# The causal mask of the row maxima moves from VectorE's reduction into a second bf16 product on TensorE

## The chip, the core and the metric

The program runs on one core of a Trainium2 chip. A core has a matrix engine (TensorE, PE in the profile, whose weight loads are the row PEld), VectorE (DVE), ScalarE (ACT), GpSimd (POOL) and a DMA-issuing engine (SP). Matrix products are written to PSUM, of which this kernel uses eight banks of 128 partitions by 512 fp32 numbers. The metric is the device time of one execution in microseconds (us). The kernel before takes 1426.77 us, the median of three runs that lie between 1425.55 and 1429.22 us.

## The reference

Two stages follow each other. The first is causal attention over 8 batches of 8 heads, with 576 positions and 64 numbers a head, and a decay that is summed along the sequence:

```python
scores = scale * np.matmul(q, k.transpose(0, 1, 3, 2))
bias = -(cum[:, :, :, None] - cum[:, :, None, :])
scores = np.where(causal, -1000000000.0, scores + np.minimum(bias, 0.0))
scores = scores - np.max(scores, axis=-1, keepdims=True)
attn = np.exp(scores)
attn = attn / (np.sum(attn, axis=-1, keepdims=True) + 1e-09)
return np.matmul(attn, v).astype(np.float32)
```

The second mixes the attention's output x with the real part of a two-dimensional Fourier transform, normalises each row, and applies a two-layer network with a hidden width of 2048:

```python
u = x + mixed
un = (u - mu) / np.sqrt(var + 1e-06)
ch = np.maximum(un @ w_ch1, 0.0) @ w_ch2
return (u + ch).astype(np.float32)
```

The change concerns one line of the first stage: the maximum of each row over the positions that the causal mask leaves.

## The kernel before

**Attention.** The 64 heads are worked in 32 steps of two heads (`i` in the loop at L585). Each step has several streams. `load` and `high` (L418, L420) and `low` (L435 on VectorE, L438 on GpSimd) split q and k into a rounded part and a remainder. `maxes` (L446 to L475) computes the rows' maxima, `scores` (L479 to L502) the exponentials with the maximum already subtracted, and `av` (L506 to L533) the product with v. `recip` and `finish` divide by the sums. For every fourth step a batch is complete, and `folds` (L244 to L268, mainly VectorE and GpSimd) and `fourier` (L274 to L342, mainly TensorE) mix it. A share of the weight conversion (`rounded`, L74 to L91) runs beside all this.

**The maxima.** For each head, the 576 query rows are cut into five blocks c of 128 rows (the last has 64). Block c needs the keys up to its own last row, so its product (L459) has 256, 256, 384 and 512 columns for c = 0 to 3; the last block has two products, of 256 and 320 columns. Each product goes into one of five PSUM buffers of the pool `psm`, which the products of `av` and the transposition of the maxima (L471) share. VectorE then reduces each buffer to one column. Where the product holds the diagonal block, a fused operation (L466) adds a mask from `amask`, writes the masked row to `trash`, and keeps the maximum in an accumulator, which a second instruction reads out into a column of `M` (`Mx` in the profile). The mask tile `amask` has 512 columns of zeros and then a 128 x 128 triangle with -1e30 above the diagonal; its window is placed so that the triangle meets the diagonal. Of the last block's two products, the first has no diagonal: a plain maximum (L462) puts it into `M1`, and that number is the starting value of the second one's accumulator. The ten columns of `M` are transposed on TensorE (L471), copied by ScalarE (L473), and sent by a DMA (L474) into row 2 of the query tile `qy`, where the products of `scores` (L491) read them.

**What sets the order.** `weave` and `mixed` (L702 to L717) take the next piece from the stream that is furthest behind its share, so the order in which the program issues is fixed when it is built. From L584 to L639 TensorE's order is exactly that order. On the other engines the framework's planner places the instructions. Each engine then runs its own queue in order and stops at an instruction whose semaphore has not come. Where `low` overwrites `k1`, VectorE waits at L435 until the last product of `scores` that reads it (L492) is done.

**Network.** After attention come the last folds, the rest of the weight conversion and the first normalisation; then nine token tiles (`mlp_tile`, L164) run products of 512 columns (L183, L196 to L198).

Of the kernel before, what the change touches and what calls it, by code (L numbers as in the profile page):

```python
# [8 lines left out]
F32 = mybir.dt.float32  # L9
F32R = mybir.dt.float32r  # L10
AF = mybir.ActivationFunctionType
ALU = mybir.AluOpType
BF16 = mybir.dt.bfloat16
I32 = mybir.dt.int32
U16 = mybir.dt.uint16
AX = mybir.AxisListType
# [9 lines left out]
NEG = -1.0e30  # L26
# [15 lines left out]
def fused_kernel(ctx, tc, qkT, vA, sP, wP, tabD, tabS, corr, out):  # L42
    nc = tc.nc
# [14 lines left out]
    ident = const.tile([128, 128], F32, name="ident")  # L58
# [289 lines left out]
    att = att_ctx.enter_context(tc.tile_pool(name="att", bufs=1, side="right"))  # L348
# [39 lines left out]
    Ms = [att.tile([128, 10], F32, name=f"Mx{i}") for i in range(2)]  # L388
    for M in Ms:
        nc.vector.memset(M, 0.0)  # L390
    amask = att.tile([128, 640], BF16, name="amask")
    nc.gpsimd.memset(amask, 0.0)
    nc.gpsimd.affine_select(out=amask[:, 512:640], in_=amask[:, 512:640], pattern=[[-1, 128]], compare_op=ALU.is_ge, fill=NEG, base=0, channel_multiplier=1)
    trash = att.tile([128, 512], BF16, name="trash")
    for i in range(1, NR):
        fixed_rows(i, nc.gpsimd, nc.gpsimd)

# [48 lines left out]
    def maxes(i):  # L446
        st = sts[i]
        qy, ky = st["qy"], st["ky"]
        M = Ms[i % 2]
        M1 = att.tile([128, 4], F32, tag="M1", name="M1", bufs=2)  # L450
        for h in range(2):
            for c in range(5):
                nq = 128 if c < 4 else 64
                nk = 128 * c + nq
                parts = [(0, max(nk, 256))] if c < 4 else [(0, 256), (256, 320)]
                col = M[:nq, 5 * h + c:5 * h + c + 1]
                for x, (k0, n) in enumerate(parts):
                    p = psm.tile([128, 512], F32, tag="m", name="pm", bufs=5)
                    nc.tensor.matmul(p[:, :n], qy[:, h, 128 * c:128 * c + 128], ky[:, h, k0:k0 + n], start=True, stop=True)  # L459
                    if len(parts) > 1 and not x:  # L460
                        first = M1[:nq, h:h + 1]
                        nc.vector.tensor_reduce(out=first, in_=p[:nq, :n], axis=AX.X, op=ALU.max)  # L462
                    else:
                        n = nk - k0
                        m0 = 512 - 128 * c + k0
                        nc.vector.tensor_tensor_reduce(out=trash[:nq, :n], in0=p[:nq, :n], in1=amask[:nq, m0:m0 + n], scale=1.0,  # L466
                                                       scalar=first if x else NEG, op0=ALU.add, op1=ALU.max, accum_out=col)
                    yield 1.0
        yield 3
        p = psm.tile([128, 512], F32, tag="m", name="pmt", bufs=5)  # L470
        nc.tensor.transpose(out=p[0:10, 0:128], in_=M, identity=ident)  # L471
        mt = att.tile([10, 128], F32R, tag="mt", name="mt", bufs=2)
        nc.scalar.copy(mt, p[0:10, 0:128])  # L473
        nc.sync.dma_start(out=qy[2:3].bitcast(F32).rearrange("o h (c t) -> o (h c) t", t=128), in_=mt.bitcast(F32))  # L474
        yield 1.0  # L475
# [95 lines left out]
    weave([high(0), 1])  # L571
    cum_rows()
    weave([low(0), 1], [high(1), 1], [maxes(0), 1.0])
    weave([low(1), 1], [high(2), 1], [maxes(1), 1.0])
    mixing = None
    weights = convert_w(attb, 0, NC, 1)
# [8 lines left out]
    for i in range(NP):  # L585
# [5 lines left out]
        if 2 <= i + 1 < NP:  # L591
            streams.append([maxes(i + 1), MAXES / 0.7])
            streams.append([later(low(i + 1), i % 4 == 0), (6, 7, 4, 3)[i % 4]])
# [69 lines left out]
    op = None  # L663
# [149 lines left out]
```

## Time and profile before

| what | value |
|---|---|
| median of three runs | 1426.77 us (1425.55 to 1429.22) |
| profiled execution | 1426.1 us, of which the span is 1424.4 us |
| mean granted TensorE clock | 0.971 |
| attention, 20 to 540 us | PE busy 446.6 us, DVE 377.9 us, mean clock 0.95 |
| between the stages, 540 to 703 us | PE busy 137.1 us, DVE 144.4 us, mean clock 0.92 |
| network, 703 to 1424.4 us | PE busy 715.8 us, DVE 207.9 us, mean clock 1.00 |
| L459, the products of the maxima | 384 matrix products |
| L466, the masked maxima | 320, each with an accumulator read |
| L462, the plain maxima | 64 |

The span runs from the first to the last instruction; the profiled execution's own time is 1.7 us longer than its span. Busy time is the time covered by an engine's instructions. TensorE's products overlap, and their recorded ends are modelled, so the step from one recorded start to the next tells more than the recorded duration. The stretches of the table come from a view that gives each engine's busy time between two times of the span, with the clock that the throttle granted.

### The profile page before, as it was taken

Reading aid. Unit: us, or ns where it says so; the run is one execution under the profiler, and the core shown is the slowest. Engines: PE = TensorE matmul, PEld = TensorE weight load, DVE = VectorE, ACT = ScalarE, POOL = GpSimd, SP = SyncE. Lnnn points to the kernel's source line nnn. Section 1 sums busy time; section 2 is a strip of 40 time slices with the busy share of each in tenths; the row PEclk is TensorE's granted clock in tenths of the full one; section 3 lists DMA queues with packets and bytes.
Section 4 is the critical chain, followed back from the end, with each engine's and each line's share of the span. In section 5 each row is a group of like instructions: output and inputs, shape, how many; then the busy total and the mean of one; then the engine's idle time right before and its main releaser. Section 6 shows DMA issues by size and latency. Waiting matters only on the chain.

```text
span 1424.4 us, 17997 instructions
## 1 busy us (share of the span) xinstructions
PE 1305.1 (92%) x6190; PEld 1068.7 (75%) x6190; DVE 745.7 (52%) x1684; ACT 539.3 (38%) x1211; POOL 561.6 (39%) x543
## 2 busy tenths in 40 slices
PE   4887979897988887997899999999999999999998
PEld 3766868686777676775688888888888888888886
DVE  6667677877777788799833233222332223322212
ACT  4775756676665656344321121211212112121110
POOL 6445465656546566565720402204022040123300
PEclk9998999999999997999899999999999999999999
DMA  8555556565655555433200000000000000000000
GB/s 214 156 159 144 163 149 180 158 168 159 159 161 144 166 149 163 162 123 121 79 8 30 31 30 15 15 30 31 30 15 15 30 30 30 15 16 0 30 0 30
DMA packets 78230, 125.05 MB, mean 88 GB/s; under 512 B 11256, under 2 KB 36249, under 8 KB 78139
## 3 DMA queue, kind: packets, MB, share of 16 engines
q1 hardware_dynamic: 75627, 119.83, 28.4%
q0 software_dynamic: 1696, 2.50, 0.9%
q10 hardware_dynamic: 816, 1.57, 0.3%
q8 instruction: 49, 0.80, 0.2%
q14 instruction: 42, 0.34, 0.1%
HBM read 76.85 MB, written 23.07 MB: 70 GB/s over the span
## 4 chain that ended last, share of the span: by engine, by line
PE 51%; DVE 7%; POOL 2%; DMA 1%; issue 1%; ACT 1%; SPq 0%; DVEq 0%; POOLq 0%; ACTq 0%
PE h L183 25%; PE acc L198 8%; PE acc L196 8%; PE acc L197 8%; POOL we L89 1%; DVE wm L88 1%; DVE we L83 1%; DVE wm L85 1%; DVE we L87 1%; DVE wl L114 1%; ACT wh L112 1%; DMA wl<-wD 0%; POOL wl L114 0%; DVE ucl L148 0%; DVE zl L188 0%
## 5 line engine op out<-in xcount | busy, mean ns | idle before, releaser
L188 DVE SCALAR_TENSOR_TENSOR zl<-h,zh 128x512 fp32r<-128x512 f32 x144 | 98.6, 686 | 405.5 <-ACT zh L187 405.4
L187 ACT ACTIVATE zh<-h 128x512 fp32r<-128x512 f32 x144 | 85.9, 596 | 530.1 <-PE h L183 530.1
L198 PE MATMUL acc<-zl,wh 128*128 128x512 f32 x576 | 227.5, 396 | 4.9 <-DVE zl L188 4.9
L196 PE MATMUL acc<-zh,wh 128*128 128x512 f32 x576 | 227.6, 395 | 1.0 <-ACT zh L187 1.0
L197 PE MATMUL acc<-zh,wl 128*128 128x512 f32 x576 | 226.8, 394 | 0.0
L523 PE MATMUL pavB<-P,va 128*128 128x320 f32 (+2 forms) x640 | 189.1, 389 | 9.5 <-ACT stage L527 8.9
L459 PE MATMUL pm<-KQ 128*128 128x256 f32 (+3 forms) x384 | 156.5, 427 | 44.4 <-DVE Mx L466 23.1
L495 ACT ACTIVATE P<-ps 128x320 f32<-128x320 f32 (+4 forms) x384 | 145.9, 393 | 110.5 <-PE ps L492 106.8
L491 PE MATMUL ps<-KQ 128*128 128x256 f32 (+2 forms) x384 | 154.1, 404 | 24.4 <-ACT P L495 14.0
L183 PE MATMUL h<-uch,wh 128*128 128x512 f32 x576 | 159.9, 398 | 8.3 <-ACT wh L112 8.3
L183 PE MATMUL h<-uch,wl 128*128 128x512 f32 x576 | 158.1, 396 | 0.8 <-DVE wl L114 0.8
L183 PE MATMUL h<-ucl,wh 128*128 128x512 f32 x576 | 156.9, 393 | 0.0
L466 DVE CUSTOM_DVE_ANT_0 trash<-pm,amask 128x128 bf16<-128x128 f32 (+3 forms) x256 | 123.5, 482 | 34.2 <-PE pm L459 16.9
L212 POOL TENSOR_TENSOR o<-o,w 128x512 f32<-128x512 f32 x32 | 41.8, 1305 | 252.3 <-issue 218.5
L183 PEld LDWEIGHTS h<-uch,wh 128*128 128x128 f32 x576 | 108.2, 190 | 35.9 <-ACT wh L112 12.1
L198 PEld LDWEIGHTS acc<-zl,wh 128*128 128x128 f32 x576 | 108.7, 189 | 32.0 <-DVE zl L188 6.9
L183 PEld LDWEIGHTS h<-uch,wl 128*128 128x128 f32 x576 | 109.2, 190 | 26.6 <-DVE wl L114 1.2
L196 PEld LDWEIGHTS acc<-zh,wh 128*128 128x128 f32 x576 | 108.6, 188 | 26.1 <-ACT zh L187 1.8
L183 PEld LDWEIGHTS h<-ucl,wh 128*128 128x128 f32 x576 | 108.9, 189 | 24.7
L197 PEld LDWEIGHTS acc<-zh,wl 128*128 128x128 f32 x576 | 108.6, 189 | 24.7
L459 PEld LDWEIGHTS pm<-KQ 128*128 128x128 f32 x384 | 78.4, 207 | 64.7 <-DVE Mx L466 30.2
L492 PE MATMUL ps<-q,k 128*128 128x256 f32 (+2 forms) x384 | 120.5, 316 | 3.1 <-POOL q L438 3.1
(140 smaller groups left out, 2066.9 us busy)
## 6 DMA issues: line engine op xcount, KB each, us to landing
qk<-in_qkT_dram SPq DMA_DIRECT2D x32, 576.0 KB
raw<-in_wP_dram SPq DMA_DIRECT2D x64, 256.0 KB
va<-in_vA_dram SPq DMA_DIRECT2D x32, 480.0 KB
q<-KQ SPq DMA_DIRECT2D x32, 288.0 KB
k<-KQ SPq DMA_DIRECT2D x32, 288.0 KB
rb<-rd SPq DMA_DIRECT2D x64, 144.0 KB
u<-uD SPq DMA_DIRECT2D x8, 1024.0 KB
out_dram<-o SPq DMA_DIRECT2D x32, 256.0 KB
```

Source lines behind the costliest of these rows:

```text
L183: nc.tensor.matmul(h[:, :n], a[:, j * 128:(j + 1) * 128], b[:, j, :n], start=i == 0, stop=i == 11)
L187: nc.scalar.activation(zh[:, :n], h[:, :n], AF.Relu)
L188: nc.vector.scalar_tensor_tensor(out=zl[:, :n], in0=h[:, :n], scalar=0.0, in1=zh[:, :n].bitcast(F32), op0=ALU.max, op1=ALU.subtract)
L196: nc.tensor.matmul(acc[j][:, :n], a[:, cs], y[:, :n], start=g == 0, stop=False)
L197: nc.tensor.matmul(acc[j][:, :n], b[:, cs], y[:, :n], start=False, stop=False)
L198: nc.tensor.matmul(acc[j][:, :n], a[:, cs], z[:, :n], start=False, stop=g == NF - 1)
L459: nc.tensor.matmul(p[:, :n], qy[:, h, 128 * c:128 * c + 128], ky[:, h, k0:k0 + n], start=True, stop=True)
L466: nc.vector.tensor_tensor_reduce(out=trash[:nq, :n], in0=p[:nq, :n], in1=amask[:nq, m0:m0 + n], scale=1.0, scalar=first if x else NEG, op0 ...
L491: nc.tensor.matmul(p[:, :n], ky[:, h, ksl], qy[:, h, a:a + n], start=True, stop=False)
L492: nc.tensor.matmul(p[:, :n], k1[:, h, ksl], q1[:, h, a:a + n], start=False, stop=True)
L495: nc.scalar.activation(P[:, o:o + a + n - lo], p[:, lo - a:n], AF.Exp, scale=0.125)
L523: nc.tensor.matmul(p[:, a - lo:n], va[:, c, vs], P[:, o:o + w], start=c == 0, stop=c == cs[-1])
```

## The change

The maxima get their mask on TensorE. A 128 x 128 bf16 triangle `above` (zero on and below the diagonal, -1e30 above it) and a bf16 unit matrix `unit` are made once at the start, in place of `amask` and `trash`. Every product that holds a diagonal block is followed by a second product, `unit` times `above`, of 128 columns (64 in the last block), which is added in PSUM onto the block's 128 diagonal columns. VectorE then takes a plain maximum of the product, for all twelve products of a step. The last block's two parts now go to separate columns, and one small VectorE operation per step combines the two heads' parts before the transposition. `M1` shrinks from four columns to two. The pieces' weights in `weave` stay as they are.

```diff
-    amask = att.tile([128, 640], BF16, name="amask")
-    nc.gpsimd.memset(amask, 0.0)
-    nc.gpsimd.affine_select(out=amask[:, 512:640], in_=amask[:, 512:640], pattern=[[-1, 128]], compare_op=ALU.is_ge, fill=NEG, base=0, channel_multiplier=1)
-    trash = att.tile([128, 512], BF16, name="trash")
+    above = att.tile([128, 128], BF16, name="above")
+    nc.gpsimd.memset(above, 0.0)
+    nc.gpsimd.affine_select(out=above, in_=above, pattern=[[-1, 128]], compare_op=ALU.is_ge, fill=NEG, base=0, channel_multiplier=1)
+    unit = att.tile([128, 128], BF16, name="unit")
+    nc.vector.tensor_copy(unit, ident)
...
-        M1 = att.tile([128, 4], F32, tag="M1", name="M1", bufs=2)
+        M1 = att.tile([128, 2], F32, tag="M1", name="M1", bufs=2)
...
                     p = psm.tile([128, 512], F32, tag="m", name="pm", bufs=5)
-                    nc.tensor.matmul(p[:, :n], qy[:, h, 128 * c:128 * c + 128], ky[:, h, k0:k0 + n], start=True, stop=True)
-                    if len(parts) > 1 and not x:
-                        first = M1[:nq, h:h + 1]
-                        nc.vector.tensor_reduce(out=first, in_=p[:nq, :n], axis=AX.X, op=ALU.max)
-                    else:
-                        n = nk - k0
-                        m0 = 512 - 128 * c + k0
-                        nc.vector.tensor_tensor_reduce(out=trash[:nq, :n], in0=p[:nq, :n], in1=amask[:nq, m0:m0 + n], scale=1.0,
-                                                       scalar=first if x else NEG, op0=ALU.add, op1=ALU.max, accum_out=col)
+                    last = x == len(parts) - 1
+                    nc.tensor.matmul(p[:, :n], qy[:, h, 128 * c:128 * c + 128], ky[:, h, k0:k0 + n], start=True, stop=not last)
+                    if last:
+                        d0 = 128 * c - k0
+                        nc.tensor.matmul(p[:, d0:d0 + nq], unit, above[:, :nq], start=False, stop=True)
+                    nc.vector.tensor_reduce(out=col if last else M1[:nq, h:h + 1], in_=p[:nq, :min(n, nk - k0)], axis=AX.X, op=ALU.max)
                     yield 1.0
+        nc.vector.tensor_tensor(out=M[:64, 4:10:5], in0=M[:64, 4:10:5], in1=M1[:64], op=ALU.max)
         yield 3
```

## The prediction

> **What bounds the kernel now.** I first read the page's busy times, then split the span into its stages, then looked for the saturated engine inside the stage that holds the maxima.
>
> ```profile
> PE 1305.1 (92%) x6190; PEld 1068.7 (75%) x6190; DVE 745.7 (52%) x1684; ACT 539.3 (38%) x1211; POOL 561.6 (39%) x543
> ```
> ```profile
> 20.00:540.00 520.00, 446.61 (x2478) 375.83 (x2478) 377.88 (x1078) 326.69 (x814) 297.48 (x309) 0.95 0.58 161
> 540.00:703.00 163.00, 137.08 (x601) 107.65 (x602) 144.44 (x298) 76.91 (x170) 96.65 (x101) 0.92 0.39 130
> 703.00:1424.40 721.40, 715.77 (x3101) 582.00 (x3099) 207.92 (x272) 125.73 (x213) 154.30 (x114) 1.00 0.06 22
> ```
>
> After its width, each row of the second view has the busy time of PE, PEld, DVE, ACT and POOL, then the granted clock. The network (from 703 us) is solid TensorE work and the change touches nothing in it; the middle stretch holds no maxima either. Both can only shift. In attention TensorE is busy for 86% and VectorE for 73% on average, and the average hides two regimes, which the same view shows in finer cuts:
>
> ```profile
> 140.00:180.00 40.00, 38.06 (x232) 32.76 (x231) 27.10 (x91) 27.80 (x70) 19.35 (x23) 1.00 0.56 157
> 280.00:320.00 40.00, 39.62 (x247) 35.34 (x247) 29.07 (x100) 27.89 (x70) 21.89 (x24) 0.99 0.64 181
> sum 240.00, PE 230.76 PEld 201.10 DVE 162.74 ACT 164.52 POOL 122.36; mean PE 32.97 PEld 28.73 DVE 23.25 ACT 23.50 POOL 17.48
> 120.00:140.00 20.00, 12.80 (x54) 10.03 (x54) 15.20 (x37) 11.32 (x28) 11.94 (x11) 0.74 0.53 142
> 180.00:200.00 20.00, 11.91 (x66) 9.62 (x65) 18.60 (x37) 10.99 (x28) 15.63 (x16) 0.88 0.48 136
> 320.00:340.00 20.00, 13.07 (x60) 10.09 (x60) 16.32 (x39) 9.94 (x27) 13.13 (x13) 0.83 0.56 169
> sum 280.00, PE 213.29 PEld 172.03 DVE 218.12 ACT 164.40 POOL 179.37; mean PE 23.70 PEld 19.11 DVE 24.24 ACT 18.27 POOL 19.93
> ```
>
> The first sum is over the seven stretches in which TensorE is saturated (100 to 120, 140 to 180, 200 to 240, 280 to 320, 340 to 380, 400 to 440, 500 to 520 us): PE busy for 230.8 of 240 us. The second is over the rest of 20 to 560 us without 40 to 60: PE 213.3 of 280 us, VectorE 218.1. There VectorE carries the folds of a finished batch, TensorE waits, and the clock falls. The waits of 20 to 540 us say who waits for whom:
>
> ```profile
> PE pm L459 <- DVE Mx L466: 22.4, 11, 5.5
> PE ps L491 <- ACT P L495: 14.0, 17, 2.2
> PE pmt L471 <- DVE Mx L466: 3.3, 2, 2.4
> DVE k L435 <- PE ps L492: 54.1, 20, 4.6
> ```
>
> TensorE waits 25.7 us in 13 places for a maximum (for a free PSUM buffer, mostly, or for the last column of `M`). VectorE waits twice as long, 54.1 us in 20 places, for TensorE's last product of a step. So TensorE sets the pace in most steps, and VectorE around the folds.
>
> **TensorE gets 320 more products** (10 a step, 32 steps), each with a load of `unit`. The trace has no bf16 product, so I bound its price. A product streams its columns while the next one's weights load. Weight loads of single instructions:
>
> ```profile
> 301.33 0.34 PEld L523 LDWEIGHTS pavB<-P,va 128*128 128x128 f32 x2
> 301.58 0.19 PEld L491 LDWEIGHTS ps<-KQ 128*128 128x128 f32 x1
> 301.70 0.19 PEld L492 LDWEIGHTS ps<-q,k 128*128 128x128 f32 x1
> ```
> ```profile
> 301.09 0.28 PE L491 MATMUL ps<-KQ 128*128 128x256 f32 x1
> 301.20 0.28 PE L492 MATMUL ps<-q,k 128*128 128x256 f32 x1
> 301.32 0.31 PE L459 MATMUL pm<-KQ 128*128 128x320 f32 x1
> 301.47 0.33 PE L523 MATMUL pavB<-P,va 128*128 128x64 f32 x2
> 301.61 0.40 PE L491 MATMUL ps<-KQ 128*128 128x320 f32 x1
> ```
>
> The long products go at 0.11 to 0.12 us per 256 columns (301.09, 301.20, 301.32). The two 64-column passes have little to stream: the whole pair takes 0.14 us from recorded start to recorded start of the next product (301.47 to 301.61), 0.07 each, and that is the low end. But a weight load starts when the previous load's weights go into use, and the loads of L491 and L492 behind the pair stand 0.12 us apart (301.58, 301.70; 0.11 before rounding). The second pass therefore held the array for 0.11 us, as long as the next full load of 128 columns. The mask product is in that position: short, with a full fp32 load behind it. I take 0.110 us; low end 0.07. The load of `unit` itself hides under the product of L459 in front of it, which lasts at least 0.11 us; without that cover the price doubles to 0.22, my high end. [...]
>
> Where does this lie on the path? The products of L459 in the saturated stretches, first and last of the seven:
>
> ```profile
> 100.00:120.00 20.00, 6.09 (x16) 2.83 (x15) 1.00 0.63 160
> 500.00:520.00 20.00, 7.66 (x21) 3.84 (x21) 1.00 0.46 130
> ```
>
> All seven hold 16+33+33+34+32+33+21 = 202 of the 384, so 202 x 320/384 = 168 mask products, 168 x 0.110 = 18.5 us. The 9.2 us in which PE is idle there (short waits for ScalarE) can cover some; I let half of it do so, 18.5 - 4.6 = **+13.9 us**. The other 152 cost 16.7 us and fall where PE is idle for 66.7 of 280 us; but after each stall TensorE runs solid again, so I count a quarter, **+4.2 us**. Were that cover gone, it would be 16.7.
>
> **VectorE gets shorter maxima.** By shape, busy time and mean duration:
>
> ```profile
> L466 DVE CUSTOM_DVE_ANT_0 trash<-pm,amask 128x256 bf16<-128x256 f32 x64 | 26.6, 416 | 10.1 <-PE pm L459 6.1
> L462 DVE TENSOR_REDUCE M<-pm 64x1 f32<-64x256 f32 x64 | 26.3, 411 | 1.9 <-PE pm L459 1.8
> L466 DVE DVE_READ_ACCUMULATOR2_ANT Mx<- 128x1 f32 x256 | 20.7, 81 | 0.0
> ```
> ```profile
> 264.61 0.42 DVE L466 CUSTOM_DVE_ANT_0 trash<-pm,amask 128x256 bf16<-128x256 f32 x1
> 264.96 0.08 DVE L466 DVE_READ_ACCUMULATOR2_ANT Mx<- 128x1 f32 x1
> 265.19 0.56 DVE L466 CUSTOM_DVE_ANT_0 trash<-pm,amask 128x384 bf16<-128x384 f32 x1
> 266.52 0.41 DVE L462 TENSOR_REDUCE M<-pm 64x1 f32<-64x256 f32 x1
> 267.07 0.54 DVE L466 CUSTOM_DVE_ANT_0 trash<-pm,amask,M 64x320 bf16<-64x320 f32 x1
> 270.11 0.41 DVE L462 TENSOR_REDUCE M<-pm 64x1 f32<-64x256 f32 x1
> 270.45 0.16 DVE L538 TENSOR_SCALAR sums<-sums 32x36 f32<-32x36 f32 x1
> ```
>
> A plain maximum of 256 columns lasts as long as a masked one (411 and 416 ns). The gain is in the succession: masked behind masked, 264.61 to 265.19, is a step of 0.58 us for 256 columns; a plain one followed by other work, 270.11 to 270.45, is 0.34. Some 0.23 us go with each masked maximum that stands behind another maximum, probably because it waits for the earlier one's write. Plain maxima write separate columns, so I expect the short step, and if they wait all the same (266.52 to 267.07 is 0.55) the gain is nothing. It counts only where TensorE waits for a maximum: 13 places, with one to six such successions in VectorE's queue ahead; three each, 13 x 3 x 0.23 = **-9.0 us** (bounds 0 and -25.7, the whole wait). Elsewhere VectorE would only wait longer at L435.
>
> The small maximum per step is new: by L538 it lasts 0.16 us or somewhat more, plus a wait for the maxima before it. Behind it stands the transposition, which waited for `Mx` in 2 of 32 steps, and the queue's next split or conversion: **+1 us**, bounds 0 and 32 x 0.35 = 11. The start-up edits (a smaller memset on POOL, one copy on VectorE) hide under the DMA waits of the first 11 us; I count 0, at most 0.5 either way.
>
> Sum: 13.9 + 4.2 - 9.0 + 1 = +10.1 us on the profiled execution's own 1426.1 us (span 1424.4 plus 1.7), 1436.2. The median of the runs is 0.7 above that execution, so I predict **1437 us**.
>
> **The rivals.**
>
> *The products cost only their streaming* (low end, 0.07): 168 x 0.07 - 4.6 = 7.2, and 152 x 0.07 / 4 = 2.7, with -9.0 and +1: +1.9 us, 1428.7. The short recorded starts at 301.47 and 301.61 speak for it, the loads against it.
>
> *The stalls for the maxima decide* (faster). VectorE reaches its folds earlier and TensorE's added work fills the rest, so the waits for `Mx` vanish whole: -25.7. The clock, which fell to 0.74, 0.88 and 0.83 in the three stall windows quoted, loses 20 x (0.26 + 0.12 + 0.17) = 11 us there; half of it returns, -5.5. With +18.1 and +1 that is -12.1, 1414.7. It decides once the relief exceeds 19.1 us. For it: the longest wait is 5.5 us and VectorE is at 18.6 of 20 there. Against it: in the longest one no maximum stands in VectorE's queue for 12 us, folds and splits alone, which do not shrink:
>
> ```profile
> 317.43 0.53 DVE L466 CUSTOM_DVE_ANT_0 trash<-pm,amask,M 64x320 bf16<-64x320 f32 x1
> 329.80 0.28 DVE L466 CUSTOM_DVE_ANT_0 trash<-pm,amask 128x128 bf16<-128x128 f32 x1
> ```
>
> [...]
>
> *VectorE gains nothing*, because the plain maxima still wait for one another: +19.1, 1445.9.
>
> *The load of `unit` is exposed too*, 0.22 us: 37.0 - 4.6 + 8.4 - 9.0 + 1 = +32.8, 1459.6.
>
> **How the numbers follow.** Forecast 0.45, streaming only 0.16, stalls decide 0.18, no relief 0.13, exposed load 0.08. A measurement of this kernel tells 0.3%, 4.3 us, from no change. Faster takes the third case and a little of the second, 0.20; the same takes most of the second and the low edge of the forecast, 0.19; slower the rest, 0.61. The range from 1417 to 1452 leaves out the end of the third case and the last one. The forecast's own is 1430 to 1445.
>
> **What would show it.** The mask products' successors should load 0.11 us behind them; 0.07 or 0.22 shows my price wrong. Plain maxima in succession should step by about 0.34 us at 256 columns. The saturated stretches should hold the same work in some 6% more time, while waits of L459 for a maximum fall from 22.4 us towards 13. If attention ends before 540 us, the third case holds; if those waits fall and attention is still longer, mine does.

## The result, and the profile after

The changed kernel takes 1451.5 us, against 1427.6 us for the kernel before on the same chip: a ratio of 1.0165, 95% interval 1.0134 to 1.0196, or +23.6 us (19.1 to 28.0). One of its four runs took 3270.7 us and is left out of the ratio as slow. The forecast was +10 us. The sign was right, the size less than half, and the time lies at the upper end of the range.

The busy times of the page after, with the added products in them:

```profile
PE 1340.7 (92%) x6510; PEld 1080.8 (75%) x6510; DVE 748.4 (52%) x1397; ACT 539.4 (37%) x1211; POOL 561.8 (39%) x543
```

TensorE is busy for 35.6 us more (1340.7 - 1305.1), which is 320 times 0.111. VectorE has 287 instructions less and is busy for 2.7 us *more*: a plain maximum is as long as a masked one (414 ns against 416 at 256 columns, 547 against 555 at 384), the accumulator reads that went (20.7 + 4.8 us by shape before) lay within the recorded time of the maxima, and the small maxima are new. The maxima by shape, after:

```profile
L466 DVE TENSOR_REDUCE Mx<-pm 128x1 f32<-128x384 f32 x64 | 35.0, 547 | 14.5 <-PE pm L465 13.5
L466 DVE TENSOR_REDUCE Mx<-pm 128x1 f32<-128x256 f32 x64 | 26.5, 414 | 9.4 <-PE pm L465 9.0
L468 DVE TENSOR_TENSOR Mx<-Mx,M 64x2 f32<-64x2 f32 x32 | 15.5, 484 | 0.6
```

After the bar stand busy time, mean ns of one, and the idle time in front of the group with its releaser. The maxima now wait for the mask product (L465). The waits of 20 to 560 us show the same thing from both sides (total, times, longest):

```profile
DVE k L437 <- PE ps L492: 69.8, 24, 4.9
DVE Mx L466 <- PE pm L465: 38.9, 62, 3.8
PE pm L462 <- DVE Mx L466: 15.1, 12, 4.6
PE pmt L471 <- DVE Mx L468: 8.2, 5, 3.0
```

TensorE's waits for a maximum fall from 22.4 to 15.1 us, as announced; the experiments below show that this fall is no evidence for the shorter maxima. The transposition's wait rises from 3.3 to 8.2, and VectorE's own wait for `scores` from 54.1 to 69.8 us. All in all TensorE waits 23.3 us for maxima where it waited 25.7.

Where in the span does the time arise? The products of the network's first layer (L183; their first and last recorded start are the two numbers behind the durations) cut it at the end of attention. Before, and then after:

```profile
L183 PE MATMUL h<-uch,wh x576: 387/395/796, 572.4 to 1410.9; 128*128 128x512 f32 x192
```
```profile
L183 PE MATMUL h<-uch,wh x576: 387/395/628, 589.4 to 1436.4; 128*128 128x512 f32 x192
```

Up to the first of them the changed kernel has lost 17.0 us, and 8.5 us more between the first and the last (847.0 against 838.5). The second part contains no maxima. The prediction had said that this stretch could only shift.

### The profile page after: what moved, and what is told of

It is laid out like the page before. It is cut to its first block, busy times and chain, and to the rows that moved or that the text cites. A ratio compares the mean times of both kernels' runs of the same rounds, so it can differ in the third digit from the quotient of the medians.

```text
span 1449.9 us, 18110 instructions
## 1 busy us (share of the span) xinstructions
PE 1340.7 (92%) x6510; PEld 1080.8 (75%) x6510; DVE 748.4 (52%) x1397; ACT 539.4 (37%) x1211; POOL 561.8 (39%) x543
## 4 chain that ended last, share of the span: by engine, by line
PE 55%; DVE 9%; ACT 2%; issue 2%; DMA 2%; POOL 1%; SPq 0%; DVEq 0%; POOLq 0%; ACTq 0%
PE h L183 25%; PE acc L196 8%; PE acc L198 8%; PE acc L197 8%; DVE we L83 1%; PE pavB L523 1%; DMA raw<-in_wP_dram 1%; DVE wm L85 1%; DVE wm L88 1%; DVE we L87 1%; POOL we L89 1%; PE pm L462 1%; DVE wl L114 1%; PE pyc L306 1%; PE ps L491 1%
## 5 line engine op out<-in xcount | busy, mean ns | idle before, releaser
L523 PE MATMUL pavB<-P,va 128*128 128x320 f32 (+2 forms) x640 | 192.6, 395 | 5.3 <-ACT stage L527 5.2
L462 PE MATMUL pm<-KQ 128*128 128x256 f32 (+3 forms) x384 | 158.9, 430 | 34.7 <-DVE Mx L466 15.1
L491 PE MATMUL ps<-KQ 128*128 128x256 f32 (+2 forms) x384 | 166.3, 435 | 21.8 <-ACT P L495 10.2
L466 DVE TENSOR_REDUCE Mx<-pm 128x1 f32<-128x128 f32 (+4 forms) x320 | 148.1, 478 | 42.7 <-PE pm L465 38.9
L183 PE MATMUL h<-uch,wh 128*128 128x512 f32 x576 | 159.4, 397 | 7.6 <-ACT wh L112 7.6
L183 PE MATMUL h<-uch,wl 128*128 128x512 f32 x576 | 158.0, 396 | 0.0
L183 PE MATMUL h<-ucl,wh 128*128 128x512 f32 x576 | 157.7, 395 | 0.0
L183 PEld LDWEIGHTS h<-uch,wh 128*128 128x128 f32 x576 | 107.6, 189 | 35.2 <-ACT wh L112 11.6
L183 PEld LDWEIGHTS h<-uch,wl 128*128 128x128 f32 x576 | 109.1, 189 | 25.4
L183 PEld LDWEIGHTS h<-ucl,wh 128*128 128x128 f32 x576 | 109.3, 190 | 24.9
L197 PEld LDWEIGHTS acc<-zh,wl 128*128 128x128 f32 x576 | 108.9, 189 | 24.6
```

The source lines that it names most:

```text
L183: nc.tensor.matmul(h[:, :n], a[:, j * 128:(j + 1) * 128], b[:, j, :n], start=i == 0, stop=i == 11)
L197: nc.tensor.matmul(acc[j][:, :n], b[:, cs], y[:, :n], start=False, stop=False)
L466: nc.vector.tensor_reduce(out=col if last else M1[:nq, h:h + 1], in_=p[:nq, :min(n, nk - k0)], axis=AX.X, op=ALU.max)
L491: nc.tensor.matmul(p[:, :n], ky[:, h, ksl], qy[:, h, a:a + n], start=True, stop=False)
L523: nc.tensor.matmul(p[:, a - lo:n], va[:, c, vs], P[:, o:o + w], start=c == 0, stop=c == cs[-1])
```

## The experiments

Four questions stood open: whether TensorE's added time or VectorE's edit makes the loss, what the 8.5 us behind attention are, why the shorter maxima bring nothing, and what one mask product costs. The added us of each run are its ratio less one, times the time of the kernel before as measured beside it. "Old order" below means the order that the planner gave the kernel before. To hold it, every instruction of an engine is tied to the one ahead of it in that order:

```python
for a, b in zip(seq, seq[1:]):      # seq: one engine's instructions
    tc.add_manual_dep(b, a.name, info, reason="order kept")
```

The tie adds no semaphore; it only leaves the planner no choice. The kernel before, tied in its own order, was not run; the nearest is the run further down in which all engines but TensorE are tied in it (1.0001). Line numbers shift by a few in these kernels.

### One part of the change at a time

**The product alone**: mask product added, masked maxima and accumulators kept.

```diff
...
-  nc.tensor.matmul(p[:, :n], qy[...], ky[...], start=True, stop=True)
+  nc.tensor.matmul(p[:, :n], qy[...], ky[...], start=True, stop=not last)
+  if last:
+      nc.tensor.matmul(p[:, d0:d0 + nq], unit, above[:, :nq], start=False, stop=True)
```

> The kernel before, with the second bf16 product behind each diagonal product, and VectorE's masked maxima kept as they were (the mask is then added twice, which no maximum notices). Measured in the changed kernel's trace: a mask product holds TensorE for 0.126 us, not 0.110. Theory (TensorE pays): with the prediction's own shares, 168 x 0.126 - 4.6 + 152 x 0.126 / 4 = +21 us over the kernel before, nearly all of the change's +24. Rival (VectorE's side or the planner's new order makes the loss): under +8 us.

Measured: 1.0156 (1.0134 to 1.0179), +22.3 us. The whole loss is there with VectorE's maxima as they were.

**The plain maximum alone**: as the changed kernel, without the mask product; the causal mask of the maxima is left out.

```diff
...
-  nc.tensor.matmul(p[:, d0:d0 + nq], unit, above[:, :nq], start=False, stop=True)
...
```

> The changed kernel without its second product: the causal mask of the maxima is left out, so that a row's maximum also covers later positions of its diagonal block. VectorE's side of the change alone. Theory (relief as predicted): -9 us against the kernel before. Rival (the small new maximum in front of the transposition takes the relief back, as the changed kernel's waits of TensorE for maxima, 22.4 + 3.3 us before and 15.1 + 8.2 after, suggest): between -3 and +2 us.

Measured: 0.9993 (0.9978 to 1.0008), -1.0 us. VectorE's half of the change is worth nothing that can be measured.

**The masked maxima without their write to one tile**: the kernel before, with `trash` in four buffers in turn.

```diff
-  trash = att.tile([128, 512], BF16, name="trash")
...
+  trash = att.tile([128, 512], BF16, tag="trash", name="trash", bufs=4)
```

> The kernel before with four tiles in turn for the masked row that nobody reads, so that a masked maximum no longer waits for the write of the one before. No work is moved to TensorE. Theory (each succession costs 0.23 us because of that write, and the relief counts where TensorE waits for a maximum): the step of two masked maxima of 256 columns falls from 0.58 to about 0.35 us, and the time by up to 9 us. Rival (the wait is the accumulator's): step and time as before.

Measured: 0.9999 (0.9975 to 1.0024). The timeline of VectorE in this run:

```profile
270.94 0.41 DVE L466 CUSTOM_DVE_ANT_0 trash<-pm,amask 128x256 bf16<-128x256 f32 x1
271.28 0.08 DVE L466 DVE_READ_ACCUMULATOR2_ANT Mx<- 128x1 f32 x1
271.28 0.55 DVE L466 CUSTOM_DVE_ANT_0 trash<-pm,amask 128x384 bf16<-128x384 f32 x1
271.75 0.08 DVE L466 DVE_READ_ACCUMULATOR2_ANT Mx<- 128x1 f32 x1
```

The step of a masked maximum of 256 columns is 0.34 us here (270.94 to 271.28), where it was 0.58 before (264.61 to 265.19), and the accumulator read runs beside the next maximum. So the 0.23 us were indeed the wait for the earlier maximum's write to the same tile, as the prediction guessed. Removing them leaves the time as it was: the relief of the masked maxima with no cost on TensorE, and still no gain (the planner's order differs a little in this run).

**Two mask products**, the second a repetition of the first.

```diff
+  nc.tensor.matmul(p[:, d0:d0 + nq], unit, above[:, :nq], start=False, stop=False)
   nc.tensor.matmul(p[:, d0:d0 + nq], unit, above[:, :nq], start=False, stop=True)
```

> The changed kernel with every mask product issued twice. Theory (TensorE pays at the margin): 320 more products, the same share exposed as for the first ones, +21 us or more over the changed kernel, so about +45 over the kernel before. If the products were hidden and the loss came from elsewhere: within 6 us of the changed kernel.

Measured: 1.0166 (1.0133 to 1.0198), +23.7 us, no more than one product. This did not fit a loss that is proportional to TensorE's work. But the planner had also ordered the other engines anew: of the 1364 VectorE instructions of the kernel before, accumulator reads aside, 1207 keep their sequence in the changed kernel. With the product alone it is 1237. Hence the next runs, which hold the order.

### The change with the order held

Four kernels: the product alone, the whole change, and the change with two products, all in the old order; and the kernel before, with no added work, in the order of the changed kernel.

> The kernel before with the 320 mask products added and the masked maxima kept, and on every engine the instructions stand in the order that the planner gave the kernel before (the added ones right behind their main products). Theory A, TensorE's added time makes the loss: by the gap of 0.126 us that the trace after shows for one mask product, 168 x 0.126 in the saturated stretches less 4.6 of cover, and a quarter of 152 x 0.126 elsewhere, +21 us, so about 1.013 to 1.017, the same as with the planner's own order. Theory B, the planner's new order on the other engines makes it: 0 to +5 us, 1.000 to 1.004.

> The whole change, with every engine in the order that the planner gave the kernel before; the small maximum stands right behind the step's last plain maximum. Theory A: +21 us less what the plain maxima save (nothing measurable in the run without mask products), so 1.012 to 1.017. Theory B: 0 to +5 us, 1.000 to 1.004.

> As the whole change in the old order, with the mask product issued twice. The pair of products held 0.182 us in the earlier run where one held 0.126. Theory A: the second product is paid like the first, 168 x 0.056 + 152 x 0.056 / 4 = +11 to +12 us above the run with one product in the old order. Theory B: TensorE's idle time takes it, at most +4 us above that run.

> The kernel before, with no added work, and on every engine its instructions in the order that the planner gave the changed kernel. Theory A: the order alone costs nothing, 0.997 to 1.003. Theory B: the order makes the loss, +15 to +24 us, 1.011 to 1.017.

| kernel | ratio (95%) | us added |
|---|---|---|
| product alone, old order | 1.0123 (1.0082 to 1.0165) | +17.6 |
| whole change, old order | 1.0104 (1.0062 to 1.0145) | +14.8 |
| two products, old order | 1.0172 (1.0128 to 1.0215) | +24.6 |
| kernel before, new order | 1.0036 (1.0009 to 1.0062) | +5.1 |

Both theories were partly right; 1.0123 and 1.0104 lie just below the ranges that the first had stated, 1.0036 just above the one that let the order cost nothing. TensorE's added time makes 15 to 18 us and the order about 5; together that is the 23.6 us of the change within its interval. With the order held, the second product is paid too: +9.8 us over one by the ratios, whose intervals overlap, and 12.6 us by the start of the network in the traces (602.6 against 590.0). The first and last product of the network's first layer separate the two parts. Product alone in the old order; whole change in the old order; kernel before in the new order:

```profile
L184 PE MATMUL h<-uch,wh x576: 387/395/796, 591.3 to 1429.9; 128*128 128x512 f32 x192
```
```profile
L184 PE MATMUL h<-uch,wh x576: 387/394/504, 590.0 to 1428.0; 128*128 128x512 f32 x192
```
```profile
L184 PE MATMUL h<-uch,wh x576: 387/395/631, 571.1 to 1417.1; 128*128 128x512 f32 x192
```

The products, in the old order, delay the end of attention by 18.9 and 17.6 us against 572.4 and add nothing behind it (838.6 and 838.0 us from first to last, before 838.5). The new order, without the products, ends attention 1.3 us earlier and adds 7.5 us behind it (846.0). The change, with 17.0 and 8.5, has about the sum of both (16.3 and 7.0). The second part separates the orders well: 835.8 to 839.5 us in all seven traces with the other engines' old order, 846.0 to 847.3 in the three with the new one. The end of attention is less steady: it lies between 571.0 and 579.9 us in the traces of the eight kernels that add nothing to TensorE, so the figures up to there hold to some us only.

**The order, split.** The kernel before with TensorE alone in the new order, and with the four other engines alone in it:

> The kernel before, no added work; TensorE alone stands in the order of the changed kernel, which from 584 us on runs twelve products of the network's first tile earlier; VectorE, ScalarE, GpSimd and SyncE keep the old order. Theory A, TensorE's earlier products wait for VectorE and hold up what follows: the stretch from the first to the last product of the network's first layer (838.5 us before, 846.0 with the whole new order) grows by 5 to 7 us, 1.003 to 1.005. Theory B, the other engines' order does it: at most 2 us, 1.000 to 1.002.

> The kernel before, no added work; VectorE, ScalarE, GpSimd and SyncE stand in the order of the changed kernel, TensorE keeps the old one. Theory A: the stretch stays within 2 us of 838.5 us. Theory B: it grows by 5 to 7 us, 1.003 to 1.005.

Measured: 1.0001 (0.9981 to 1.0022) for TensorE's, 1.0040 (1.0024 to 1.0056), +5.7 us, for the others'. The first layer's products, in the same sequence:

```profile
L184 PE MATMUL h<-uch,wh x576: 387/395/796, 574.0 to 1412.7; 128*128 128x512 f32 x192
```
```profile
L184 PE MATMUL h<-uch,wh x576: 387/395/797, 571.0 to 1418.3; 128*128 128x512 f32 x192
```

838.7 and 847.3 us: it is the order of VectorE, ScalarE, GpSimd and SyncE. In that stretch they convert the weights and serve the network's first tile at once. Waits of TensorE in it, from 560 us to its end, kernel before and then the run with the others' new order:

```profile
PE acc L198 <- DVE zl L188: 4.9, 4, 2.7
```
```profile
PE acc L199 <- DVE zl L189: 7.7, 6, 2.5
PE pzs L285 <- ACT Do L70: 3.8, 1, 3.8
```

TensorE waits 2.8 us longer for VectorE's `zl` of the network, and once 3.8 us for ScalarE's part of the last fold, which did not stand among its waits of this stretch before. The second cannot make the loss, since it is only 1.2 us in the run with the whole new order, whose stretch is about as long. In all, TensorE is idle for 5.5 us more between the first layer's first and last product (24.6 us against 19.1). The other 3.3 us are longer busy time of the same products (822.7 against 819.4 us), with a granted clock of 0.93 until 711 us against 0.95 until 705 us. Which pair of instructions changed places to cause it was not tried.

### The relief by itself

The plain maxima in the old order, no product (the causal mask of the maxima is again left out):

> The plain maxima and the small maximum without any mask product (the causal mask of the maxima is left out), every engine in the order that the planner gave the kernel before: the relief by itself, since TensorE has no added work and nothing is rearranged. Theory A, the prediction's step: -9.0 + 1 = -8 us, 0.994 (as far as -25 us if all waits of TensorE for a maximum vanish), with the waits of the main products for a maximum falling from 22.4 us towards 13. Theory B, the relief is hidden because those waits end with work ahead of the maxima in VectorE's queue: within 2 us of the kernel before, 0.998 to 1.002.

Measured: 1.0018 (1.0002 to 1.0034), +2.6 us. Not even the order hides a gain: there is none, and with the small maximum it is rather a small loss. VectorE's timeline in this run shows the short step, 0.33 us at 256 columns (268.40 to 268.73):

```profile
268.40 0.41 DVE L464 TENSOR_REDUCE M<-pm 64x1 f32<-64x256 f32 x1
268.73 2.24 DVE L464 TENSOR_REDUCE Mx<-pm 64x1 f32<-64x320 f32 x5
```

And yet the waits, from 20 to 560 us, hardly move (before 22.4 in 11 places). VectorE itself waits longer for the products of the maxima, 32.4 us instead of 20.2.

```profile
PE pm L463 <- DVE Mx L464: 19.9, 10, 4.8
```

The timeline of VectorE says why. It ends with the maximum for which TensorE waited 4.8 us (from 330.90 to 335.72); the same place, 5.5 us long, in the kernel before ends with L466 at 329.80.

```profile
331.00 0.94 DVE L71 TENSOR_TENSOR De<-Df,De 128x289 fp32r<-128x289 f32 x1
331.97 0.77 DVE L267 TENSOR_TENSOR eh<-e,eh 1x289 fp32r<-1x289 f32 x1
332.77 0.94 DVE L261 TENSOR_TENSOR Df<-Bw 128x288 f32<-128x288 f32 x1
333.74 0.75 DVE L438 TENSOR_TENSOR k<-qk,KQ 64x576 fp32r<-64x576 f32 x1
334.52 0.94 DVE L71 TENSOR_TENSOR Do<-Df,Do 128x288 fp32r<-128x288 f32 x1
335.38 0.28 DVE L464 TENSOR_REDUCE Mx<-pm 128x1 f32<-128x128 f32 x1
```

Folds and a split stand ahead of one single maximum. In the kernel before, the five longest waits of the products (5.5, 4.3, 3.1, 2.9 and 2.6 us, 18.4 of the 22.4) have only one maximum, in one case two, in VectorE's queue between their begin and their end. Beside it stand folds and splits, in the third the reciprocals of the sums.

Then why do these waits fall to 15.1 us in the changed kernel? The run with the product alone in the old order has the old masked maxima and shows it too:

```profile
PE pm L466 <- DVE Mx L476: 13.2, 8, 4.8
```

One might think that TensorE's added work brings it later to the same buffer. But the run with TensorE alone in the new order (1.0001) has no added work and masked maxima, and from 30 to 580 us every engine runs the sequence of the kernel before:

```profile
PE pm L460 <- DVE Mx L467: 16.2, 9, 4.8
PE pmt L472 <- DVE Mx L467: 6.1, 3, 2.8
```

So the same work in the same order shows 22.4 us of the products' waits in one trace and 16.2 in another, at profiled times of 1426.1 and 1427.9 us, and 3.3 and 6.1 us for the transposition. In the place of the longest wait the two splits of VectorE ahead of the maximum took 1.49 and 1.24 us in the kernel before (L435 at 323.88 and 328.15) and 0.87 and 0.75 in this run. A fall from 22.4 to 15.1 us in one trace is therefore evidence neither for a faster VectorE nor for a later TensorE; that there is no gain rests on the times of the runs.

### The price of one product

> The whole change in the old order, with unit and above (and so the mask product) in the 32-bit type of the main product instead of bf16. Theory A, the change of type between neighbours is what keeps the load of unit from starting under the main product: the load now starts under it as the other loads do, the gap of one mask product falls from 0.126 us to 0.06 to 0.11 us, and the loss from +15 us to +8 to +13. Theory B, it is not the type: the gap stays at 0.12 us or becomes longer (a 32-bit product of 128 columns may stream more slowly), and the loss is +15 us or more.

```diff
...
-  above = att.tile([128, 128], BF16, name="above")
-  unit = att.tile([128, 128], BF16, name="unit")
+  above = att.tile([128, 128], F32R, name="above")
+  unit = att.tile([128, 128], F32R, name="unit")
```

The same place in four kernels: a main product of 512 columns and then a product of `av` (L523 or L524). The granted clock there is 1.00 in the kernel before, and in all four the next product starts 0.23 us behind the main one. First the loads (PEld) and products (PE) of the kernel before; then of the change, with two products, and with the 32-bit product, all in the old order:

```profile
203.86 0.39 PE L459 MATMUL pm<-KQ 128*128 128x512 f32 x1
204.09 0.49 PE L523 MATMUL pavB<-P,va 128*128 128x192 f32 x2
...
203.86 0.42 PEld L523 LDWEIGHTS pavB<-P,va 128*128 128x128 f32 x2
```
```profile
208.58 0.39 PE L463 MATMUL pm<-KQ 128*128 128x512 f32 x1
208.81 0.23 PE L466 MATMUL pm<-above,unit 128*128 128x128 bf16 x1
208.87 0.54 PE L524 MATMUL pavB<-P,va 128*128 128x192 f32 x2
...
208.80 0.10 PEld L466 LDWEIGHTS <-unit 128*128 128x128 bf16 x1 [0.15 <-issue]
208.81 0.31 PEld L524 LDWEIGHTS pavB<-P,va 128*128 128x128 f32 x2
```
```profile
213.26 0.10 PEld L466 LDWEIGHTS <-unit 128*128 128x128 bf16 x1 [0.16 <-issue]
213.28 0.10 PEld L467 LDWEIGHTS <-unit 128*128 128x128 bf16 x1
```
```profile
211.64 0.39 PE L463 MATMUL pm<-KQ 128*128 128x512 f32 x1
211.87 0.22 PE L466 MATMUL pm<-above,unit 128*128 128x128 f32 x1
...
211.64 0.19 PEld L466 LDWEIGHTS pm<-above,unit 128*128 128x128 f32 x1
211.87 0.30 PEld L524 LDWEIGHTS pavB<-P,va 128*128 128x128 f32 x2
```

In these rows a 32-bit load starts together with the product ahead of it (203.86 and 203.86; 211.64 and 211.64); in the trace before, 5482 of 6189 loads start within 10 ns of that product and none earlier. The bf16 load of `unit` is recorded 0.22 us later than the main product (208.80 against 208.58), just before its own product starts (208.81): by the record nothing of it is hidden. In all 320 places of the changed kernel's trace it stands only 3 to 5 ns ahead of its own product, where the 32-bit load stands 0.23 us ahead (211.64 and 211.87). The mask product itself starts about 0.23 us behind the main product with either type (208.81 and 211.87), as `av` does without one (204.09), so the late load delays it by a few ns at most (0.232 against 0.228 us, lower quartiles of 24 places each in the traces after and before). The time from the start of the main product to the start of the second pass of `av` behind it, the lower quartile over all places of this kind (24 in each), is 0.390 us without a mask product, 0.517 with one, 0.572 with two and 0.502 with the 32-bit one. So one bf16 product costs 0.127 us, the second 0.055, the 32-bit one 0.112. Of the 0.127 us, 0.066 lie between the mask product and the first pass of `av`, and 0.057 are a longer first pass (0.218 us against 0.161); with the 32-bit product it is 0.059 and 0.052. Most of the price is thus paid whether the load of `unit` is hidden or not. If both types stream alike, which no run shows, the late load is worth the difference, 0.015 us.

The expectation of the first theory holds for the load and nearly for the price (0.112 us, where 0.06 to 0.11 was expected), not for the time: 1.0120 (1.0089 to 1.0151), +17.1 us, against +14.8 with the bf16 product. The difference, 320 x 0.015 = 5 us at most, of which by the other runs about half would be paid, is lost in the intervals.

By the recorded starts, a 32-bit load starts with the product in front of it, be that a 32-bit one (211.64) or a bf16 one (208.81 and 208.81; within 10 ns in 291 of 320 places of the trace after). The bf16 load behind a bf16 product is recorded 0.02 us behind that product's start (213.28 against 213.26, with two products), the one behind a 32-bit product of 512 columns 0.22 us behind it.

### Another order

The kernel with two products lost no more than the one with a single one, so its planner's order might be the better one. The kernel before, and the change, in that order:

> The kernel before, no added work, with every engine in the order that the planner gave the kernel with two mask products. That kernel lost 18.7 us up to the end of attention in its own order and 32.9 us in the old one, so its order saved 14 us there. Theory A, the order is better for this work whatever the mask costs: attention ends some 5 to 14 us earlier, 0.990 to 0.997. Theory B, the order only fits where TensorE is the later engine: 0.998 to 1.005.

> The whole change, one mask product, with every engine in the order that the planner gave the kernel with two. Theory A, TensorE's second product was paid in that order too, 11 to 14 us for 320 x 0.056: the loss falls to +10 to +14 us, 1.007 to 1.010, below the +15 us in the order of the kernel before. Theory B, that order had room for the second product: +20 to +24 us, as the change in its own order.

Measured: 1.0014 (0.9997 to 1.0032) and 1.0158 (1.0128 to 1.0188), +22.6 us. Neither is a gain. In this order the first product costs about 20 us and the second about 1 (23.7 - 22.6); in the old one they cost 15 and 10. The second theory of the last expectation fits. But each of these figures has an interval of 4 us and more to either side, so whether the two orders really share the cost differently stays open. No version was found that beats the kernel before.

## Why the prediction was right or wrong

**TensorE's two terms were right in size, +18.1 us.** The product alone in the old order, which holds just these terms, added 17.6 us by the runs (11.7 to 23.6) and 18.9 in the trace. If each of the 6190 products is paired with its counterpart in the trace before, the delay grows by 13.7 us inside the seven saturated stretches (forecast 13.9, and 5.7% of their 240 us where 6% were announced) and by about 5 us in the rest of 20 to 560 us (forecast 4.2). So close a match of the two parts is luck: paired in the same way, the whole change in the old order gives 15.7 and 0.8 us, and the run with TensorE alone in the new order, which adds nothing, -2.0 and +2.7. The sum is borne out, the split is not.

**The price was nearly right, by a reason that held in the main.** 0.110 us was argued from a short product with a full 32-bit load behind it, the load of `unit` hidden. For a 32-bit mask product just that was measured, 0.112. For the bf16 product the load is not hidden by the record, and the price is 0.127 us. The rival in which the exposed load costs 0.22 us foresaw the late load, but not its size: with 0.112 us for a hidden one there are 0.015 us left for it. The announced sign, successors that load 0.11 us behind, could not be read: the next load is recorded 5 to 6 ns behind that of `unit` in 290 of 320 places, because that one comes late itself (208.80 and 208.81). The 0.11 us was read from the distance of two loads as if each had started with the product in front of it, but they stand 0.06 and 0.08 us behind the recorded starts of the products in front of them (301.58 against 301.53, 301.70 against 301.61), so it was an estimate and no clean reading. With 0.127 the prediction's own formula gives 168 x 0.127 - 4.6 + 152 x 0.127 / 4 = 21.6 us, more than the 17.6 measured but inside its interval. Whether the shares of idle time taken as cover were right is therefore not shown.

**The step that failed: the relief of VectorE, -9.0 us.** Its length was right (0.58 us before; 0.34 with the rotated tiles, 0.33 with plain maxima). Its count was not: three successions were put ahead of every wait, and where TensorE waited long there were other operations, folds and splits mostly, and one maximum. The prediction saw that for the longest wait, quoted it against the faster rival, and did not apply it to its own term. In place of -9.0 us the runs showed nothing, its bound of 0: together with the small maximum -1.0 us (-3.1 to +1.1) in one order and +2.6 (0.3 to 4.9) in the other. The rival "VectorE gains nothing" gave 1445.9 us; the change in the old order took 1444.5. Its number fits, its reason (the plain maxima still wait for one another) does not. The rival "the stalls decide" had 5.5 us of clock return with shorter stalls. No run shows that term: from 20 to 560 us the mean granted clock was 0.95 before and 0.95 in the changed kernel, where TensorE waited 25.7 and 23.3 us for maxima, and over the whole span it was 0.961 to 0.971 in the runs with the plain maximum alone, 0.959 to 0.971 in the runs of the kernel before beside them.

**The cost that was missing: the planner's new order, about +5 us.** The prediction treated everything outside attention as shifted. It had named the planner as what places the instructions of the other engines, and gave no term to the fact that 320 more products and 287 fewer VectorE instructions make it place them anew, in parts of the program that the change does not touch.

**The small maximum, +1 us**, is not settled by a run of its own. Of its 32 instructions, 22 take 0.15 to 0.16 us, as was taken; ten are recorded with 0.7 to 1.4 us. The transposition waits 4.9 us more in the changed kernel (8.2 against 3.3), but it also waits 6.1 us in the run with TensorE alone in the new order, without a small maximum, so at most a part of that growth is the small maximum's. The start-up edits at 0 were not tried by themselves.

**The announced sign was a weak one.** "Those waits fall and attention is still longer" came true, but the product alone does that without any relief, and the waits fall to 16.2 us even where nothing is changed in that stretch. A sign must differ between the theories that it is to tell apart.

In short: 17.6 for the products, nothing or up to 3 us for VectorE's half instead of -8, and 5 for the order make the 23.6 us, where 18.1 - 9.0 + 1 had been written.

## What to carry to other kernels

Before a relief is credited against a wait, read which instructions stand in the releasing engine's queue from the begin of that wait to its end; only those that become shorter count (here one maximum, in one case two, in each of the five longest waits). Take a second trace of the unchanged kernel before a change in a sum of waits is read at all (here 22.4 and 16.2 us). Where a planner orders the queues, a local edit can have a second cost with no local place (here 5.1 us): run the edit with the old order held, and the old kernel in the new order, before the loss is put down to the edit. And ask which engine sets the pace: here 320 products added to TensorE cost 17.6 us by themselves, while the shorter maxima of VectorE alone brought no gain (+2.6 us) and its waits for the products of the maxima grew from 20.2 to 32.4 us.

## What the runs showed of the hardware

The bf16 load of `unit` behind a 32-bit product of 512 columns was recorded 0.22 us after that product's start, with 0.15 us of TensorE's load side idle, and in all 320 places of the changed kernel's trace 3 to 5 ns ahead of its own product; a 32-bit load in the same place started with the product in front (211.64). One bf16 mask product between 32-bit ones cost 0.127 us, a 32-bit one 0.112, and the second of two bf16 products 0.055; that the late load makes the difference between the first two is not shown. A masked maximum of 256 columns that writes its unused row to the same tile as its forerunner stepped 0.58 us to the next one, and 0.34 us with tiles in turn, 0.24 us less; the read of its accumulator, 0.08 us, ran beside the next maximum in that run. The step of a plain maximum was 0.33 us. The sum of TensorE's waits for maxima differed between two traces of the same work in the same order by 6 us (22.4 and 16.2), at profiled times of 1426.1 and 1427.9 us.
